# Narrow first FFN groups, one fp32 load, reordered loads, a DMA queue model and new durations in a statically scheduled attention + SwiGLU kernel

## The chip, the cores and the metric

One core of one Trainium2 chip. The metric is device time of one execution in microseconds (us); the median of several executions is quoted, and versions are compared by ratios of runs taken in the same rounds on the same chip. PE is TensorE, PEld its weight loads, DVE VectorE, ACT ScalarE, POOL GpSimd, SP SyncE.

## The reference, cut to what matters

```python
# q, k, v: [4, 8, 768, 64]; window 128, 4 sink keys; x: [3072, 512]
scores = q @ k.T / sqrt(64), kept where (key < 4) or (0 <= query - key < 128)
attn   = softmax(scores) @ v
x      = attn laid out as [tokens, heads * 64]
xn     = x / sqrt(mean(x * x) + 1e-6) * rms_g
out    = (silu(xn @ w_gate) * (xn @ w_val)) @ w_out      # 512 -> 1536 -> 512
```

The work is cut into 24 blocks of 128 tokens. Six groups of four blocks go through the FFN. For a block, attention needs its own q, k, v and those of its neighbour, and ends in `xr`, the normalized row block, which is transposed to `xnt` for the FFN.

## The kernel before: the parts concerned

The kernel does not issue instructions in the order in which it is written. It hands every piece of work to a `Plan` with a duration, what it needs and gives, and a priority. The plan plays the program through with these durations and so fixes each engine's order, once, when the program is built. On the chip every engine then works its list in order: when the first instruction of the list is not ready, the engine stands, whatever stands behind it.

```python
class Plan:
    def land(self, ring, at, work):              # when a DMA lands, as the plan believes
        others = max([v for r, v in self.rings.items() if r != ring], default=0)
        begin = max(at, self.rings.get(ring, 0))
        shared = min(work, max(0, others - begin))
        end = begin + work + shared
        ...
    def run(self):
        ...                                      # earliest start first, then priority
        free[e] = start + ns                     # ns: the duration given with the work
        if o["ring"] is not None:
            end = self.land(o["ring"], end, o["work"]) + 550
```

The loads and constants:

```python
    F32_LOADS = 2;  PE_MASKS = 2;  X_DMA_FROM = 8;  QK_DMA_FROM = 12
    GATE_LEAD = 3;  T_LEAD = 5;    GB_PRIO = -5
    # q0, q1 on SP, k0, k1 on ACT as fp32, cast by DVE; all others on GpSimd, cast by the DMA:
    for g in range(F32_LOADS): sw_block(g, "v")
    sw_w(0, 2); sw_block(2); sw_block(3)
    sw_w(2, 4); sw_w(4, 6); sw_w(6, 9); sw_w(9, 12)      # strips of w_gate and w_val
    sw_block(4); sw_wo(0, 6); sw_wo(6, 12)
    for g in range(5, NB): sw_block(g)
```

Some durations, and the FFN of a group (`ft` is one of twelve strips of 128 hidden columns; `ffn` needs `xnt` of every block in `cols`):

```python
    pe((240, 480, 590)[min(t, 2)], lambda: av(g, u), ...)       # ns
    dve(430, lambda: normal(g, u), ...)
    dve(1650, lambda: rms(g), ...)
    ...
    for G in range(NG):
        if G == 0:                                # one block at a time, four strips
            for tb in range(GB):
                for i in range(FTN // 4):
                    ffn(G, 3 * tb + i, range(4 * i, 4 * i + 4), slice(tb * P, (tb + 1) * P), ...)
        else:                                     # four blocks at once, one strip
            for ft in range(FTN):
                ffn(G, ft, (ft,), slice(0, GN), ...)
```

The softmax here doesn't subtract the row's maximum and nothing guards it: scores larger than these inputs give would overflow.

## Time and profile before

| | before |
|---|---|
| time, median of 4 runs | 257.19 us (256.48 to 257.77) |
| span of the profiled run (an execution of 257.9 us, 0.7 above the median) | 256.2 us |
| PE work, by columns at the spacing of the chain | 225.5 us |
| idle PE | 30.7 us |
| DVE, ACT, POOL busy | 183.6, 130.7, 93.1 us |

The table's PE work is not the busy time of the page: it is every listed matmul at the spacing that the chain shows (the prediction works it out). Its difference to the span is what a better order can win at most. The page's summary of the chain that ended last shows that a third of that chain is not PE. That third is no measure of idle PE (30.7 of 256.2 us): PE can have other work while the chain is on DVE.

```profile
PE 66%; DVE 21%; ACT 5%; issue 3%; DMA 2%; ACTq 0%; DVEq 0%
```

### The profile page before, as it was taken

To read this page: it belongs to the slowest core of one execution; us is meant where nothing else is said; L and a number is where in the kernel's file an instruction comes from. 1 tells how busy PE (TensorE), PEld (TensorE's weight loads), DVE (VectorE), ACT (ScalarE), POOL (GpSimd) and SP (SyncE) were. 2 spreads that over 40 slices of the span, in tenths; PEclk is the share of its full clock that TensorE was granted. 3 is DMA by queue.
4 is the path that set the end of the run, shared out by engine and by line. 5 is a ranking of instruction groups with operands and counts; after the bars stand their busy time and mean duration, and the time that the engine had idled before them with its cause. 6 is when DMAs were issued, how large, how long until landed. Compare 5 with 4: busy or idle time off the path is not lost.

```text
span 256.2 us, 5083 instructions
## 1 busy us (share of the span) xinstructions
PE 238.7 (93%) x1880; PEld 130.8 (51%) x1906; DVE 183.6 (72%) x481; ACT 130.7 (51%) x273; POOL 93.1 (36%) x128
## 2 busy tenths in 40 slices
PE   5788999989998999999989999999999989999994
PEld 1357997776544445344445444445455544444441
DVE  3577999599889998278997169998089984277600
ACT  2376463898835733446643455562564452333211
POOL 8984454989847464003303031013033310000000
PEclk9999999999999999999999999999999999999999
DMA  8999999999999999943303524301311112200012
GB/s 158 173 176 202 184 207 163 154 199 155 117 174 168 125 155 155 177 132 65 63 0 64 163 63 64 61 0 40 128 41 23 22 20 64 111 12 0 3 53 111
DMA packets 106970, 26.55 MB, mean 104 GB/s; under 512 B 97217, under 2 KB 103873, under 8 KB 106946
## 3 DMA queue, kind: packets, MB, share of 16 engines
q0 software_dynamic: 77568, 13.64, 71.6%
q1 hardware_dynamic: 27298, 12.07, 22.5%
q10 hardware_dynamic: 2080, 0.52, 1.1%
q8 instruction: 15, 0.25, 0.4%
q14 instruction: 9, 0.07, 0.1%
HBM read 28.31 MB, written 6.29 MB: 135 GB/s over the span
## 4 chain that ended last, share of the span: by engine, by line
PE 66%; DVE 21%; ACT 5%; issue 3%; DMA 2%; ACTq 0%; DVEq 0%
PE o L770 21%; PE g L737 19%; PE v L737 17%; DVE xr L547 4%; DVE p L750 3%; DVE r L543 3%; DVE hT L760 3%; DVE x L515 3%; ACT e L452 2%; PE s L439 2%; DMA stage<-in_k_dram 2%; PE av L503 2%; DVE e L469 2%; PE av L498 1%; ACT sq L523 1%
## 5 line engine op out<-in xcount | busy, mean ns | idle before, releaser
L737 PE MATMUL g<-xnt,wg 128*128 128x512 bf16 (+1 forms) x427 | 69.4, 307 | 3.7 <-DVE p L750 2.7
L737 PE MATMUL v<-xnt,wv 128*128 128x512 bf16 (+1 forms) x422 | 70.6, 306 | 0.6
L750 DVE SCALAR_TENSOR_TENSOR p<-th,g 128x512 bf16<-128x512 bf16 x72 | 48.0, 683 | 28.5 <-ACT th L744 28.5
L770 PE MATMUL o<-wo,hT 128*128 128x512 bf16 x278 | 65.6, 379 | 0.7 <-issue 0.3
L744 ACT ACTIVATE th<-g 128x512 bf16<-128x512 f32 x72 | 42.5, 599 | 34.2 <-PE g L737 31.9
L452 ACT ACTIVATE e<-s 128x512 bf16<-128x512 f32 (+1 forms) x100 | 47.2, 556 | 13.6 <-PE s L439 13.5
L737 PEld LDWEIGHTS <-wg 128*128 128x128 bf16 x432 | 33.9, 98 | 30.0 <-issue 4.8
L760 DVE TENSOR_TENSOR hT<-p,v 128x512 bf16<-128x512 bf16 x72 | 47.8, 682 | 1.9 <-PE v L737 1.3
L737 PEld LDWEIGHTS <-wv 128*128 128x128 bf16 x432 | 33.1, 98 | 24.0 <-issue 0.8
L474 POOL TENSOR_SCALAR_AFFINE_SELECT e<-e 128x512 bf16<-128x512 bf16 x20 | 12.6, 634 | 87.5 <-ACT e L452 60.5
L770 PEld LDWEIGHTS <-hT 128*128 128x128 bf16 x288 | 27.1, 98 | 30.9 <-issue 0.8
L523 ACT ACTIVATE sq<-x 128x512 bf16<-128x512 bf16 x24 | 15.1, 629 | 36.5 <-DVE x L515 36.4
L778 ACT ACTIVATE osb<-o 128x512 f32<-128x512 f32 x24 | 14.3, 606 | 26.0 <-PE o L770 26.0
L312 POOL DMA_DIRECT2D k<-in_k_dram x22 | 19.5, 889 | 11.9 <-DMA wo<-in_moe_w_out_dram 3.1
L316 POOL DMA_DIRECT2D v<-in_v_dram x24 | 21.4, 894 | 6.6 <-DMA q<-in_q_dram 3.8
L312 POOL DMA_DIRECT2D q<-in_q_dram x22 | 19.6, 891 | 7.4 <-DMA wo<-in_moe_w_out_dram 2.6
L515 DVE TENSOR_TENSOR x<-av,rden 128x256 bf16<-128x256 f32 x48 | 20.4, 425 | 1.7
L547 DVE SCALAR_TENSOR_TENSOR xr<-x,r,gb 128x512 bf16<-128x512 bf16 x24 | 18.4, 765 | 0.9
L503 PE MATMUL av<-v,e 128*128 128x65 bf16 x192 | 17.4, 197 | 1.1 <-DVE e L469 0.8
L503 PEld LDWEIGHTS <-e 128*128 128x128 bf16 x192 | 13.4, 101 | 4.7 <-DVE e L469 2.3
L498 PE MATMUL av<-v,e 128*128 128x65 bf16 x160 | 15.5, 195 | 0.0
L469 DVE TENSOR_TENSOR e<-e,masks 128x1024 bf16<-128x1024 bf16 (+1 forms) x24 | 14.9, 642 | 0.7 <-ACT e L452 0.6
(69 smaller groups left out, 181.3 us busy)
## 6 DMA issues: line engine op xcount, KB each, us to landing
out_dram<-osb SPq DMA_DIRECT2D x24, 256.0 KB, 2.0
v<-in_v_dram POOLq DMA_DIRECT2D x24, 128.0 KB, 9.1
q<-in_q_dram POOLq DMA_DIRECT2D x22, 128.0 KB, 9.8
k<-in_k_dram POOLq DMA_DIRECT2D x22, 128.0 KB, 9.0
wo<-in_moe_w_out_dram POOLq DMA_DIRECT2D x2, 768.0 KB, 15.3
wg<-in_moe_w_gate_dram POOLq DMA_DIRECT2D x3, 256.0 KB, 6.6
wv<-in_moe_w_val_dram POOLq DMA_DIRECT2D x3, 256.0 KB, 7.1
wg<-in_moe_w_gate_dram POOLq DMA_DIRECT2D x2, 384.0 KB, 11.1
```

The lines of the kernel that those rows point to most:

```text
L312: nc.gpsimd.dma_start(out=T[name, g], in_=block_of(src, g))
L316: nc.gpsimd.dma_start(out=V16[b][:, t, :, 0:D], in_=block_of(v, g))
L452: nc.scalar.activation(out=T["e", g, u][:, 2 * hi:2 * hi + 2, n0:n1, :].rearrange("p x n c -> p x (n c)"), in_=ps.rearrange("p (j c) -> p ...
L469: nc.vector.tensor_tensor(out=ev, in0=ev, in1=mv, op=ALU.mult)
L503: nc.tensor.matmul(out=dest, lhsT=T["e", g, u][:, x, 0, :], rhs=V16[b][:, t, h, :], start=(t == 0), stop=True, skip_group_check=True,)
L515: nc.vector.tensor_tensor(out=T["x16", g][:, 4 * u:4 * u + 4, :], in0=pvv[:, :, 0:D], in1=rden.unsqueeze(2).to_broadcast((P, 4, D)), op=AL ...
L547: nc.vector.scalar_tensor_tensor(out=T["xr", g], in0=T.pop(("x16", g)).rearrange("p h d -> p (h d)"), scalar=r[:, 3:4], in1=gb, op0=ALU.mu ...
L737: nc.tensor.matmul(out=ps[:, i * n:(i + 1) * n], lhsT=w_sb[:, kt, ft * P:(ft + 1) * P], rhs=T["xnt", G][:, kt, cols], start=(kt == 0), sto ...
L744: nc.scalar.activation(out=T["th", key], in_=BANK[("g", key)], func=ACT.Tanh, scale=0.5,)
L750: nc.vector.scalar_tensor_tensor(out=T["p1", key], in0=T.pop(("th", key)), scalar=1.0, in1=BANK.pop(("g", key)), op0=ALU.add, op1=ALU.mult,)
L760: nc.vector.tensor_tensor(out=T[hk][:, i:i + n, cols], in0=T.pop(("p1", key)).rearrange("p (n c) -> p n c", n=n), in1=BANK.pop(("v", key)) ...
L770: nc.tensor.matmul(out=BANK[("o", G, tb)], lhsT=T["h", G, ft // 4][:, ft % 4, tb * P:(tb + 1) * P], rhs=wo[:, ft, :], start=(ft == 0), sto ...
```

## The change: intent and diff

The intent: let the FFN of groups 1 and 2 start when two of their four blocks are ready; take fp32 casts off DVE; bring loads in the order of need; let the plan know that transposing DMAs queue behind the loads, and give it truer durations.

```diff
-    F32_LOADS = 2
-    PE_MASKS = 2
+    F32_LOADS = ("q0",)
+    LOADS = "k-0 v-0 qk-1 w-0-2 qkv-2 v-1 w-2-5 qkv-3 w-5-9 w-9-12 qkv-4 wo-0-6 qkv-5 wo-6-12 qkv-6 ..."
+    PE_MASKS = 3
-    X_DMA_FROM = 8
-    QK_DMA_FROM = 12
+    X_DMA_FROM = 10
+    QK_DMA_FROM = 10
-    GATE_LEAD = 3
-    T_LEAD = 5
+    GATE_LEAD = 2
+    T_LEAD = 3
-    GB_PRIO = -5
+    CHUNKS = (4,2,2)
+    GB_PRIO = -1200
     ...
     def land(self, ring, first, work):
+        r = self.rings
+        if ring == "POOL":                       # loads: behind each other and behind the fp32 load
+            r["POOL"] = max(first, r["POOL"], r["HW"]) + work
+            self.loads -= 1
+            return r["POOL"] + 520
+        ...
+        begin = max(first, r["TR"], r["POOL"])   # transposes and stores: behind the loads
     ...
-            dve(335, lambda: cast(n, g), ...)
+            act(640, lambda: cast(n, g, nc.scalar.copy), ...)
-            pe(270 * (n1 - n0) + 30, lambda: scores(g, *n), ...)
+            pe(220 * (n1 - n0), lambda: scores(g, *n), ...)
-            pe((240, 480, 590)[min(t, 2)], lambda: av(g, u), ...)
+            pe((130, 242, 354)[min(t, 2)], lambda: av(g, u), ...)
-            dve(430, lambda: normal(g, u), ...)
+            dve(548, lambda: normal(g, u), ...)
-        dve(1650, lambda: rms(g), ...)
+        dve(1745, lambda: rms(g), ...)
     ...
-        if G == 0: ...
-        else: ...
+        nc_ = CHUNKS[G] if G < len(CHUNKS) else 1
+        w, n = GN // nc_, 0
+        for c in range(nc_):
+            for ft in range(0, FTN, nc_):
+                ffn(G, n, range(ft, ft + nc_), slice(c * w, (c + 1) * w), p0 + 10 * n)
+                n += 1
```

Cut: bookkeeping of rings, durations of single loads, where the small GpSimd selects stand between the loads, and three added dependencies (the gb matmul waits for the first scores, a mask group for the transposes of its own q and k, the sink copy for the next block's scores). No run below takes the selects' places or these dependencies back.

More of the change, by code (lines that the diff above doesn't have):

```diff
@@ L27 @@
 class Plan:
+    LATE = 300
     HOP = {"PE": 40, "ACT": 35, "DVE": 35, "POOL": 90, "SP": 60}
@@ L36, in __init__ @@
     def __init__(self):
-        self.ops, self.given, self.rings, self.held = [], {}, {}, {}
+        self.ops, self.held = [], {}
+        self.rings = {"POOL": 0, "HW": 0, "TR": 0}
         self.banks = {i: 0 for i in range(8)}
@@ L45, in op, with land @@
         ))
-    def land(self, ring, at, work):
-        others = max([v for r, v in self.rings.items() if r != ring], default=0)
-        begin = max(at, self.rings.get(ring, 0))
-        shared = min(work, max(0, others - begin))
-        end = begin + work + shared
-        for r, v in self.rings.items():
-            if r != ring and v > begin:
-                self.rings[r] = v + shared
-        self.rings[ring] = end
-        return end
+    def land(self, ring, first, work):
+        r = self.rings
[3 more added lines that the diff above has]
+            return r["POOL"] + 520
+        if ring == "HW":
+            r["HW"] = max(first, r["HW"]) + work
+            return r["HW"] + 900
+        begin = max(first, r["TR"], r["POOL"])
+        if self.loads:
+            r["POOL"] = max(r["POOL"], first) + work
+            work *= 2
+        r["TR"] = begin + work
+        return r["TR"] + (350 if ring == "TR" else 650)
     def run(self):
-        free, given, users = dict(self.START), {}, {}
+        free, users = dict(self.START), {}
+        self.loads = sum(o["ring"] == "POOL" for o in self.ops)
         wait = {o["at"]: set(o["needs"]) for o in self.ops}
@@ L108, in run @@
             if o["ring"] is not None:
-                end = self.land(o["ring"], end, o["work"]) + 550
+                end = self.land(o["ring"], end, o["work"]) + self.LATE
             for s in o["drops"]:
@@ L158 @@
     inv_sqrt_d = 1.0 / math.sqrt(D)
-    F32_LOADS = 2
-    PE_MASKS = 2
+    F32_LOADS = ("q0",)
+    POOL_AT = (0,2,6)
+    DEPTH = 8
+    LOADS = "k-0 v-0 qk-1 w-0-2 qkv-2 v-1 w-2-5 qkv-3 w-5-9 w-9-12 qkv-4 wo-0-6 qkv-5 wo-6-12 qkv-6 qkv-7 qkv-8"
+    LOADS += "".join(f" qkv-{g}" for g in range(9, NB))
+    PE_MASKS = 3
     POOL_MASK_FROM = 12
-    X_DMA_FROM = 8
-    QK_DMA_FROM = 12
+    X_DMA_FROM = 10
+    QK_DMA_FROM = 10
     LD = 16
     GATE_FROM = 8
-    GATE_LEAD = 3
-    T_LEAD = 5
+    GATE_LEAD = 2
+    T_LEAD = 3
     SPLIT = (0,)
-    GB_PRIO = -5
+    CHUNKS = (4,2,2)
+    GB_PRIO = -1200
     const = ctx.enter_context(tc.tile_pool(name="const", bufs=1))
@@ L224, in sp @@
     def sp(ns, lat, fn, *args, **kw):
-        op({"SP": (ns, lat, fn)}, *args, ring="SP", **kw)
+        op({"SP": (ns, lat, fn)}, *args, **kw)
     dve(70, lambda: nc.vector.memset(ident, 0.0), gives=["id0"], prio=-99)
@@ L261, in spread_masks @@
         nc.vector.memset(masks[0:NS, 0, :, :], 1.0)
-    pool(270, make_ident, ["id0"], ["ident"], -90)
+    pool(270, make_ident, ["id0"], ["ident"], -89.2 + POOL_AT[0])
     for i in range(2):
         pool(270, lambda i=i: triangle(bias[:, i, :], NEG, i), ["bias0"],
-             [("bias", i)], -89.9 + i / 10)
+             [("bias", i)], -89.1 + POOL_AT[1] + i / 100)
         pool(330, lambda i=i: triangle(masks[:, 1, i, :], 0.0, i), ["masks0"],
-             [("masks1", i)], -81 + i / 10)
+             [("masks1", i)], -89.1 + POOL_AT[2] + i / 100)
     dve(220, cut_ident, ["ident"], ["idnos"], -50)
@@ L290, in make_headm @@
             )
-    pool(200, make_sel, ["sel0"], ["sel"], -80)
-    pool(180, lambda: make_headm(0), ["headm0"], ["headm1"], -79)
-    pool(180, lambda: make_headm(1), ["headm1"], ["headm"], -78)
+    pool(200, make_sel, ["sel0"], ["sel"], -89.1 + POOL_AT[2] + 1)
+    pool(180, lambda: make_headm(0), ["headm0"], ["headm1"], -89.1 + POOL_AT[2] + 2)
+    pool(180, lambda: make_headm(1), ["headm1"], ["headm"], -89.1 + POOL_AT[2] + 3)
     def block_of(src, g):
@@ L304, in load_f32, with cast @@
         eng.dma_start(out=T["st", name, g], in_=block_of(src, g))
-    def cast(name, g):
+    def cast(name, g, copy):
         T[name, g] = ld.tile([P, H, D], BF16, name=name)
-        nc.vector.tensor_copy(out=T[name, g], in_=T.pop(("st", name, g)))
+        copy(out=T[name, g], in_=T.pop(("st", name, g)))
     def load_bf16(name, src, g):
@@ L320 @@
     wo_src = moe_w_out.rearrange("(ft p) d -> p ft d", p=P)
-    sp(370, 1200, lambda: nc.sync.dma_start(
-        out=grow, in_=moe_rms_g.rearrange("(o d) -> o d", o=1)), (), ["grow"], -91, work=50)
-    for g in range(F32_LOADS):
-        sp(370, 1300, lambda g=g: load_f32("q", q, g, nc.sync), (), [("qst", g)], -90 + g,
-           work=900)
-        op({"ACT": (100, 1300, lambda g=g: load_f32("k", k, g, nc.scalar))}, (), [("kst", g)],
-           -90 + g, ring="ACT", work=900)
-        for n in "qk":
-            dve(335, lambda n=n, g=g: cast(n, g), [(n + "st", g)], [(n, g)], -9 + g)
+    for i, name in enumerate(F32_LOADS):
+        n, g = name[0], int(name[1:])
+        src, first, fn = q if n == "q" else k, i % 2 == 0, load_f32
+        if first:
+            op({"ACT": (450, 1000, lambda n=n, src=src, g=g: load_f32(n, src, g, nc.scalar))},
+               (), [(n + "st", g)], -90 + i, ring="HW", work=970)
+        else:
+            sp(400, 1000, lambda n=n, src=src, g=g: load_f32(n, src, g, nc.sync),
+               (), [(n + "st", g)], -90 + i, ring="HW", work=970)
+        act(640, lambda n=n, g=g: cast(n, g, nc.scalar.copy), [(n + "st", g), "table"],
+            [(n, g)], -99)
+    sp(400, 1000, lambda: nc.sync.dma_start(
+        out=grow, in_=moe_rms_g.rearrange("(o d) -> o d", o=1)), (), ["grow"], -89.5, ring="HW", work=50)
     act(1290, None, (), ["table"], -80)
@@ L336, in sw_load @@
         n = len(issue)
-        more = [("sw", n - 8)] if n >= 8 else []
-        op({"POOL": (ns, 1750, fn)}, list(needs) + more, list(gives) + [("sw", n)], -89 + n,
+        more = [("sw", n - DEPTH)] if n >= DEPTH else []
+        op({"POOL": (ns, 1720, fn)}, list(needs) + more, list(gives) + [("sw", n)], -89 + n,
            ring="POOL", work=work)
@@ L345, in sw_block @@
             if n == "v":
-                sw_load(lambda g=g: load_v(g), [("v", g)], 900)
+                sw_load(lambda g=g: load_v(g), [("v", g)], 910)
             else:
                 src = q if n == "q" else k
-                sw_load(lambda n=n, src=src, g=g: load_bf16(n, src, g), [(n, g)], 880,
+                sw_load(lambda n=n, src=src, g=g: load_bf16(n, src, g), [(n, g)], 860,
                         needs=[(n + "T", old)] if old >= 0 else [])
@@ L356, in sw_w @@
                 out=w_sb[:, :, cols], in_=src[:, :, cols]),
-                [(n, ft) for ft in range(f0, f1)], 650 * (f1 - f0), 740)
+                [(n, ft) for ft in range(f0, f1)], 663 * (f1 - f0), 740)
     def sw_wo(f0, f1):
@@ L361, in sw_wo @@
         sw_load(lambda: nc.gpsimd.dma_start(out=wo[:, rows, :], in_=wo_src[:, rows, :]),
-                [("wo", ft) for ft in range(f0, f1)], 650 * (f1 - f0), 810)
-    for g in range(F32_LOADS):
-        sw_block(g, "v")
-    sw_w(0, 2)
-    sw_block(2)
-    sw_block(3)
-    sw_w(2, 4)
-    sw_w(4, 6)
-    sw_w(6, 9)
-    sw_w(9, 12)
-    sw_block(4)
-    sw_wo(0, 6)
-    sw_wo(6, 12)
-    for g in range(5, NB):
-        sw_block(g)
+                [("wo", ft) for ft in range(f0, f1)], 663 * (f1 - f0), 810)
+    for what in LOADS.split():
+        n, *f = what.replace("-", " ").split()
+        if n == "w":
+            sw_w(int(f[0]), int(f[1]))
+        elif n == "wo":
+            sw_wo(int(f[0]), int(f[1]))
+        else:
+            sw_block(int(f[0]), n)
     def unit_gb():
@@ L385, in scale_gb @@
         nc.scalar.mul(gb, BANK.pop(("gb",)), C3)
-    pe(864, unit_gb, ["ones", "grow"], ["gbm"], GB_PRIO, takes=[("gb",)], mode=2)
+    pe(864, unit_gb, ["ones", "grow", ("s", 0, 0)], ["gbm"], GB_PRIO, takes=[("gb",)], mode=2)
     act(490, scale_gb, ["gbm", "table"], ["gb"], drops=[("gb",)])
@@ L646 @@
             else:
-                sp(1250, 1700, lambda n=n, g=g: dma_t(n, g),
-                   [(n, g)] + old + [("s", g - T_LEAD)], [(n + "T", g)], g, work=700)
+                sp(1290, 1200, lambda n=n, g=g: dma_t(n, g),
+                   [(n, g)] + old + [("s", g - T_LEAD)], [(n + "T", g)], g,
+                   ring="TR", work=1000)
         slots = [("s", g, u, hi) for u in range(2) for hi in range(2)]
@@ L653 @@
             pe(864, lambda g=g: mask_bias(g), [("bias", 0), ("bias", 1), "ident", "idnos"]
-               + ([("qp", g - 1)] if g else []), [("mb", g)], pa, takes=slots)
+               + ([("qp", g), ("kp", g)] if g else []), [("mb", g)], pa, takes=slots)
         for n0, n1 in parts:
@@ L658 @@
             last = (n0, n1) == parts[-1]
-            pe(270 * (n1 - n0) + 30, lambda g=g, n=(n0, n1): scores(g, *n), needs,
+            pe(220 * (n1 - n0), lambda g=g, n=(n0, n1): scores(g, *n), needs,
                [("s", g, n0)] + ([("s", g)] if last else []), pa + 1 + n0,
@@ L688 @@
             needs += [("av", g - 1, u)] if g else []
-            pe((240, 480, 590)[min(t, 2)], lambda g=g, u=u: av(g, u), needs, [("av", g, u)],
+            pe((130, 242, 354)[min(t, 2)], lambda g=g, u=u: av(g, u), needs, [("av", g, u)],
                pa + 5, takes=[("av", g, u)])
-            dve(430, lambda g=g, u=u: normal(g, u),
+            dve(548, lambda g=g, u=u: normal(g, u),
                 [("av", g, u)] + ([("xr", g - 3)] if g >= 3 else [])
@@ L696 @@
             early)
-        dve(1650, lambda g=g: rms(g),
+        dve(1745, lambda g=g: rms(g),
             [("ms", g), "gb"] + ([("xt", g - 3)] if g >= 3 else [])
@@ L709 @@
         else:
-            sp(1250, 1700, lambda g=g: dma_x(g), [("xr", g)] + old, [("xt", g)], g - 8, work=700)
+            sp(1290, 1200, lambda g=g: dma_x(g), [("xr", g)] + old, [("xt", g)], g - 8, ring="TR",
+               work=1000)
         if t == 0:
             dve(600, lambda b=b: sink_k(b),
-                [("kT", g)] + ([("ss", b - 2, i) for i in ((2, 4) if b - 2 < 2 else (2,))]
+                [("kT", g), ("s", g + 1)] + ([("ss", b - 2, i) for i in ((2, 4) if b - 2 < 2 else (2,))]
                                if b >= 2 else []), [("ksk", b)], 0.1 * g)
@@ L803 @@
         p0 = 1000.0 * G
-        if G == 0:
-            for tb in range(GB):
-                for i in range(FTN // 4):
-                    ffn(G, 3 * tb + i, range(4 * i, 4 * i + 4), slice(tb * P, (tb + 1) * P),
-                        p0 + 10 * (3 * tb + i))
-        else:
-            for ft in range(FTN):
-                ffn(G, ft, (ft,), slice(0, GN), p0 + 10 * ft)
+        nc_ = CHUNKS[G] if G < len(CHUNKS) else 1
[4 more added lines that the diff above has]
+                n += 1
         mine = [key for key in keys if key[0] == G]
@@ L815 @@
                 part = [("h", key) for key in mine if 4 * i <= key[1] < 4 * i + 4
-                        and (G or key[2] == tb * P)]
+                        and key[2] <= tb * P < key[2] + w]
                 pe(864, lambda G=G, tb=tb, i=i: project(G, tb, i),
@@ L825 @@
                 [("osb", G, tb)], drops=[("o", G, tb)])
-            sp(370, 1000, lambda G=G, tb=tb: store(G, tb), [("osb", G, tb)], [("st", G, tb)],
-               -100, work=700)
+            sp(400, 1000, lambda G=G, tb=tb: store(G, tb), [("osb", G, tb)], [("st", G, tb)],
+               -100, ring="ST", work=870)
     order = plan.run()
```

## The prediction

> **What bounds the kernel now.** I read the page first (engine shares, 40 slices), then the chain in order of time, the DMA view of the first 20 us, and engine sums in 16 us stretches.
>
> The page, engine shares and slices:
>
> ```profile
> PE 238.7 (93%) x1880; PEld 130.8 (51%) x1906; DVE 183.6 (72%) x481; ACT 130.7 (51%) x273; POOL 93.1 (36%) x128
> ...
> PE   5788999989998999999989999999999989999994
> ...
> DVE  3577999599889998278997169998089984277600
> ...
> DMA  8999999999999999943303524301311112200012
> ```
>
> PE looks full, but one 128x512 matmul is recorded as 379 ns while the chain spaces four of them at 0.86 us, so 0.215 us each. I therefore count PE work by columns: every matmul that the program lists, at the spacing the chain shows (0.215 us per 512 columns, 0.54 us for the eight score matmuls of a block, 0.03 us for a 65-column av). The sum is 225.5 us, 186 of it the three FFN products. The span is 256.2 us, so about 31 us are idle PE. To find where, I took each milestone's time from the trace and subtracted the PE work that stands ahead of it in program order: 13.5 us lost at the first g matmul (21.0 us minus 7.5), 15.0 when the third run of weight strips starts (30.5 minus 15.5), 15.5 at the first o (41.3), 19.3 at the first g of group 1 (71.0 minus 51.7), 21.7 at its first o (96.3), 22.8 and 24.0 at the same points of group 2, then only 2.9 more until the last matmul. The last 3.8 us are evacuation and store. So: **15 us at the start, 8.5 between 41 and 135 us, 3 later, 3.8 tail.** What fills the first two? The chain, cuts of it:
>
> ```profile
> 1.26 5.61 DMA stage<-in_k_dram
> ...
> 9.10 1.02 DVE q L308
> ...
> 11.90 1.82 PE s L421 x4
> ...
> 17.05 0.76 DVE xr L547
> ...
> 24.66 1.00 PE g L737 x16
> ...
> 53.02 0.75 DVE xr L547
> 55.10 0.76 DVE xr L547
> ...
> 69.27 0.75 DVE xr L547
> 70.02 0.61 DVE e L469
> 71.06 0.97 PE g L737 x4
> ```
>
> The reader is to see a serial beginning (fp32 q and k loads, casts, mask matmuls before av, normalization) and, from 45 to 71 us, DVE finishing xr of blocks 5 to 7, which the 512-column matmuls of group 1 wait for. The engine sums (columns PE, PEld, DVE, ACT, POOL) say DVE has no room then: 15.34 of 16 us, after 12.38 in the stretch before.
>
> ```profile
> 32.00:48.00 16.00, 15.79 (x223) 12.48 (x223) 12.38 (x29) 9.19 (x19) 9.66 (x12) 1.00 1.88 179
> 48.00:64.00 16.00, 14.97 (x223) 12.04 (x224) 15.34 (x46) 14.53 (x35) 14.63 (x17) 1.00 2.41 172
> ```
>
> The DMA view of 0 to 20 us:
>
> ```profile
> GB/s 0 0 0 17 134 274 287 267 218 217 219 217 212 170 155 156 175 198 187 193 201 185 156 154 156 154 156 154 154 156 153 161 191 197 193 200 197 193 199 196
> DMA packets 15089, 3.40 MB, mean 170 GB/s; under 512 B 12551, under 2 KB 15088, under 8 KB 15089
> ```
>
> Nothing moves before 1.5 us, then the DMA engines never rest: about 280 GB/s for fp32 blocks, 154 for cast blocks, 200 for weights.
>
> **What the Trainium skill says.** "Perfetto Trace Analysis", Identifying the Most-Contended Engine: matmul busy share is no measure of distance to the roofline, since matmuls are pipelined. Agrees: 379 ns recorded against 215 spaced. "TensorE: Matmul & The Clock Gate", Part 1: start to start is N/2.4 GHz + 2.5 ns warm (55.6 ns at 128 columns, 215.7 at 512), N/1.2 GHz cold. Agrees: sixteen 128-column matmuls in 0.89 us (56 ns), four 512-column ones in 0.86; the early mask group took 1.82 us, 455 ns each, so cold. That is why narrow chunks cost PE nothing. "DMA: Bandwidth & Descriptors", Issuing engines are not separate DMA queues: all issuers share the same 16 DMA engines. Agrees: busy tenths are 9 with one or three issuers. "Perfetto Trace Analysis", Optimization Strategy: where regimes change, interleaving them may help; that is what the chunks do.
>
> **The change part by part**, from the two programs' instruction order.
>
> *PE work.* Groups 1 and 2 get two chunks of 256 columns: 192 more matmuls and weight loads, same columns, 0 us by the spacing above. One more mask matmul group +0.86, two more x transposed on PE +0.43, blocks 10 and 11 of q and k no longer transposed there -0.86. Sum **+0.4 us**.
>
> *DVE and ACT.* The DVE casts of q0, k0, q1, k1 go (0.938, 0.564: 3.0 us), as do two masks of block 2 (0.686 each: 1.4); an fp32 copy of q0, an estimate of 0.6 us from the 0.59 us copies, goes to ACT. About 4 us of DVE work leave the first 25 us.
>
> *Head.* Before, first scores run at 10.7 us, and av of block 0 waits in program order behind mask group 1 until 13.5. After, q0 is the only fp32 load; at 280 GB/s its 0.26 MB are there near 3.7 us, and k0, second in line at 154 GB/s, near 5. Then q1 (issued about 3.7, landing at least 3.1 later as the fastest k load did), its transpose and copy, gb (2.07 us cold in the trace), the second half of the scores: av of block 0 near 9.8. The chain before needs 4.3 us from av to the transpose of xr, so x is ready near 14 instead of 17.9. But g and v need weight strips 0 to 4. Walking the queue with 0.94 us per fp32 block, 0.85 per cast block and 0.64 per weight strip of one matrix: before, 15.7 us of loads end with strips 2 and 3, at 17.6 from a start at 1.9, while 3.40 MB at 20 us put the same 3.15 MB at about 18.8; I add 1.2 us. After: q0 0.94, four blocks 3.4, four strips 2.56, four blocks 3.4, six strips 3.84: 14.1, so 17.2 for the last strip and 15.3 for its wg half. **First g near 16, not 21.** The gain then shrinks: the next strips (5 to 8) come behind block 3, at 22.3 and 24.9, and wg of strips 9 to 11 at 26.8. With 0.5 us to be seen, the third run of strips starts near 27.5 with 16.2 us of PE work ahead of it: 11.3 lost against 15.0. **Worth 3.5 us** (rounded down).
>
> *Chunks.* Group 1 starts on blocks 4 and 5. Adding DVE instructions in program order at their means, 61 us stand before xr of block 7 in the old program and 44 before xr of block 5 in the new one, while PE work ahead is alike (51.7 and 50.8). With that, DVE is ready by about 55 us (44, scaled by 0.91 for overlapping records as 183.6 union to 202 sum, plus some 14 idle), and PE would arrive at 51 + 12 = 63. So the 3.8 us lost there should fall to about 1.3: **worth 2.5**. From there through group 2's first o, 4.7 are lost; DVE work is only shifted earlier, so I give back a third: **1.5**. Later groups are unchunked and tail is same: 0.
>
> *Queue order, scheduler constants, DMA transposes from block 10 with shorter lead.* PE later lost only 2.9 us in 120, so I count 0.
>
> Sum: 3.5 + 2.5 + 1.5 - 0.4 = 7.1; 256.9 - 7.1 = **249.8 us**.
>
> **Rivals.** (1) *The weight stream takes the place of the fp32 loads*: three cast blocks cost 2.55 us where fp32 ones cost 2.8, so the same bytes gate group 0 and the start gains nothing but order. For it: DMA tenths of 9 until 109 us. Against: the old first g waited for xr, not for a landing. Then about 253. (2) *DVE stays the bound to 96 us*: chunks only move the wait from xr to hT, since DVE was at 15.2 of 16 again from 80 to 96. For it: p and hT need 1.2 us per 1.73 of PE, plus attention. Against: 4 us of DVE work gone and idle DVE before 48. Then about 252. (3) *All goes well*: block order and the truer queue model also close the later 2.9 us; then 246. (4) *Late transposes*: a lead of 3 blocks instead of 5 makes scores wait for landings, up to 9 us seen among them; 1 to 3 us back.
>
> **Range and chances.** Full effect 246, both rivals together about 255; 8 in 10 between 246 and 254. The 2% line is 251.8, two microseconds above my number, so faster 0.70, same 0.28, slower 0.02.
>
> **What would show it.** Right: first g near 16, 128-column g of strips 8 to 11 near 27.5, first 256-column g near 63 to 65, about 23 us idle PE in all, PE work 226. Wrong: first g waiting on weights beyond 19; DVE above 15 of 16 from 48 to 96 with g waiting on p; score matmuls waiting for transposed q or k after 80 us.

## The result, and the profile after

The changed kernel takes 250.26 us (249.8 to 250.32, 4 runs) against 257.19 us in the same rounds: ratio 0.9728, 95% interval 0.9699 to 0.9757. Ratios are the mean time of one kernel's fast runs over that of the other's fast runs of the same rounds, so not quite the ratio of the medians. The predicted time was 249.8 us, range 246 to 254. All four runs are fast ones at a granted clock of 0.997 or more.

The page of the changed kernel, in the order of the lines shown for before (shares, PE, DVE and DMA slices, chain):

```profile
PE 238.1 (96%) x2094; PEld 148.6 (60%) x2094; DVE 177.8 (72%) x470; ACT 133.2 (54%) x277; POOL 95.0 (38%) x129
...
PE   3998999999999999999999999999999999999993
...
DVE  2375879699899996599986089997279993377700
...
DMA  9999999999999999994122533212501102200022
...
PE 85%; DMA 8%; POOL 4%; issue 1%; ACT 0%; DVE 0%; POOLq 0%
```

DVE's share of the chain fell from 21% to nothing; its busy time fell by 5.8 us, but it is 72% of the span in both. PE's busy time is the same (238.7 and 238.1): busy time told nothing of the 7.7 us. The weight loads' busy time rose by 18 us for the 192 added ones, without any cost. The engine sums (PE, PEld, DVE, ACT, POOL, clock, DMA) of the stretches shown for before, and all waits of PE between 40 and 135 us:

```profile
32.00:48.00 16.00, 15.59 (x223) 12.20 (x221) 12.73 (x30) 11.04 (x23) 9.57 (x11) 1.00 1.86 181
48.00:64.00 16.00, 16.00 (x214) 12.02 (x213) 14.48 (x46) 13.88 (x32) 15.08 (x18) 1.00 2.38 166
```

The list of PE's waits for 40 to 135 us is empty. Where the idle time went, by the prediction's ledger (time of a milestone in the trace, minus the PE work ahead of it in program order, gives idle PE up to there):

| idle PE up to, us | before | after | saved in between |
|---|---|---|---|
| first g | 21.0 - 7.5 = 13.5 | 17.9 - 7.0 = 10.9 | 2.6 |
| third run of weight strips | 30.5 - 15.5 = 15.0 | 29.2 - 16.2 = 13.0 | -0.6 |
| first o of group 0 | 41.3 - 25.8 = 15.5 | 42.4 - 28.0 = 14.4 | -0.9 |
| first g of group 1 | 71.0 - 51.7 = 19.3 | 66.0 - 50.8 = 15.2 | 3.0 |
| first o of group 1 | 96.3 - 74.6 = 21.6 | 91.5 - 75.6 = 15.8 | 1.7 |
| first g of group 2 | 109.2 - 86.4 = 22.7 | 103.8 - 87.7 = 16.2 | 0.7 |
| first o of group 2 | 134.9 - 110.9 = 23.9 | 129.1 - 112.2 = 16.8 | 0.6 |
| last matmul | 252.4 - 225.5 = 26.9 | 244.6 - 225.9 = 18.7 | 1.1 |

(Each value is rounded by itself, so a difference can be 0.1 off, here and against the prediction's figures; the last column is taken from the rounded idle times.) The start gave little, 41 to 135 us gave 6.0, the rest 1.1. What changed at group 1 shows in the times of xr of blocks 6 and 7 and of the first g of group 1 (start, duration, engine, line, what), now:

```profile
63.10 0.75 DVE L560 SCALAR_TENSOR_TENSOR xr<-x,r,gb 128x512 bf16<-128x512 bf16 x1
65.99 1.91 PE L752 MATMUL g<-xnt,wg 128*128 128x256 bf16 x16
69.34 0.75 DVE L560 SCALAR_TENSOR_TENSOR xr<-x,r,gb 128x512 bf16<-128x512 bf16 x1
```

xr of block 7 is ready no earlier than before (70.1 us, 70.0 before), but the first g no longer waits for it: it starts at 66.0 us, not 71.0. The start's DMA view for 0 to 20 us explains part of how little the start gave:

```profile
GB/s 0 0 0 24 197 256 83 116 111 97 114 97 103 110 129 127 126 154 175 166 178 169 169 159 155 153 156 156 162 182 199 204 198 204 203 205 182 168 154 156
DMA packets 13252, 2.85 MB, mean 142 GB/s; under 512 B 11203, under 2 KB 13251, under 8 KB 13252
```

One column is 0.5 us. From 3.0 us on, when the single fp32 block is all but in (it lands at 3.6 us), the queue of cast loads moves 83 to 129 GB/s until 8.5 us, not 154; the kernel before moved 3.40 MB in these 20 us. The DMA busy tenths of the page read 9 all the while. The other part is the path of x of block 0, from its transpose to the first g:

```profile
16.59 0.39 PE L575 MATMUL x<-ident,xr 128*128 128x128 bf16 x4
17.01 0.42 DVE L581 COPY xnt<-x 128x512 bf16<-128x512 bf16 x1 [0.98 <-PE x L575]
17.86 1.06 PE L752 MATMUL g<-xnt,wg 128*128 128x128 bf16 x16
```

The copy to xnt ends at 17.43 us and the w_gate part that the first g needs lands at 17.62: both hold the first g, within 0.2 us of each other.

### The profile page after: what moved, and what is told of

It is laid out like the page before. It is cut to its first block, busy times and chain, and to the rows that moved or that the text cites. A ratio compares the mean times of both kernels' runs of the same rounds, so it can differ in the third digit from the quotient of the medians.

```text
span 248.5 us, 5479 instructions
## 1 busy us (share of the span) xinstructions
PE 238.1 (96%) x2094; PEld 148.6 (60%) x2094; DVE 177.8 (72%) x470; ACT 133.2 (54%) x277; POOL 95.0 (38%) x129
## 3 DMA queue, kind: packets, MB, share of 16 engines
q1 hardware_dynamic: 26306, 11.81, 22.7%
## 4 chain that ended last, share of the span: by engine, by line
PE 85%; DMA 8%; POOL 4%; issue 1%; ACT 0%; DVE 0%; POOLq 0%
PE o L785 25%; PE v L752 24%; PE g L752 23%; DMA k<-in_k_dram 5%; PE s L452 4%; DMA wv<-in_moe_w_val_dram 3%; PE av L516 2%; PE av L511 2%; PE av L501 1%; PE ss L618 1%; POOL v L331 1%; POOL k L327 1%; POOL q L327 1%; PE x L575 1%; PE k L412 1%
## 5 line engine op out<-in xcount | busy, mean ns | idle before, releaser
L752 PE MATMUL v<-xnt,wv 128*128 128x128 bf16 (+2 forms) x528 | 72.5, 282 | 0.3 <-DMA wv<-in_moe_w_val_dram 0.3
L752 PE MATMUL g<-xnt,wg 128*128 128x128 bf16 (+2 forms) x528 | 70.3, 282 | 0.1
L752 PEld LDWEIGHTS <-wg 128*128 128x128 bf16 x528 | 43.1, 98 | 19.5 <-issue 1.6
L465 ACT ACTIVATE e<-s 128x512 bf16<-128x512 f32 (+1 forms) x100 | 48.4, 551 | 10.2 <-PE s L452 10.1
L752 PEld LDWEIGHTS <-wv 128*128 128x128 bf16 x528 | 42.4, 98 | 18.2 <-issue 1.1
L785 PEld LDWEIGHTS <-hT 128*128 128x128 bf16 x288 | 26.9, 98 | 30.0 <-issue 0.8
L487 POOL TENSOR_SCALAR_AFFINE_SELECT e<-e 128x512 bf16<-128x512 bf16 x20 | 13.8, 697 | 80.9 <-ACT e L465 54.6
L793 ACT ACTIVATE osb<-o 128x512 f32<-128x512 f32 x24 | 14.5, 603 | 26.1 <-PE o L785 25.9
L327 POOL DMA_DIRECT2D q<-in_q_dram x23 | 20.6, 895 | 11.6 <-DMA wo<-in_moe_w_out_dram 3.2
L327 POOL DMA_DIRECT2D k<-in_k_dram x24 | 21.4, 892 | 8.7 <-DMA v<-in_v_dram 3.0
L536 ACT ACTIVATE sq<-x 128x512 bf16<-128x512 bf16 x24 | 15.2, 632 | 16.7 <-DVE x L528 16.4
L452 PE MATMUL s<-qkT 64*128 64x256 bf16 (+1 forms) x200 | 14.4, 266 | 0.8 <-DVE qkT L419 0.5
L511 PE MATMUL av<-v,e 128*128 128x65 bf16 x160 | 14.8, 193 | 0.0
L527 DVE RECIPROCAL rden<-av 128x4 f32<-128x4 f32 x48 | 8.4, 176 | 8.1 <-PE av L516 8.0
```

The costliest lines, as they stand in the source:

```text
L327: nc.gpsimd.dma_start(out=T[name, g], in_=block_of(src, g))
L452: nc.tensor.matmul(out=BANK[slot][:, j * 256 + n0 * P:j * 256 + n1 * P], lhsT=qkT[pr, 1, hp, t * P:(t + 1) * P], rhs=qkT[pr, 0, hp, (t + n ...
L465: nc.scalar.activation(out=T["e", g, u][:, 2 * hi:2 * hi + 2, n0:n1, :].rearrange("p x n c -> p x (n c)"), in_=ps.rearrange("p (j c) -> p ...
L511: nc.tensor.matmul(out=dest, lhsT=T["e", g - 1, u][:, x, 1, :], rhs=V16[b][:, t - 1, h, :], start=(t == 1), stop=False, skip_group_check=True,
L752: nc.tensor.matmul(out=ps[:, i * n:(i + 1) * n], lhsT=w_sb[:, kt, ft * P:(ft + 1) * P], rhs=T["xnt", G][:, kt, cols], start=(kt == 0), sto ...
L785: nc.tensor.matmul(out=BANK[("o", G, tb)], lhsT=T["h", G, ft // 4][:, ft % 4, tb * P:(tb + 1) * P], rhs=wo[:, ft, :], start=(ft == 0), sto ...
```

## The experiments

Twelve kernels were run, each correct and each timed against the kernel before on its chip. A word on what such a run can say: every edit makes the plan lay out all engines anew. Taking a part out shows what the rest is worth without it, not what the part is worth by itself, and the values do not add up. The runs are from several sessions on different chips; the kernel before took 257.19 us beside the changed kernel and 256.85, 256.57 and 256.52 beside the others, so a difference of two medians of the table can be 0.7 us off. The ratios are not touched by this.

| kernel | time, us | ratio to before (95%) |
|---|---|---|
| changed | 250.26 | 0.9728 (0.9699 to 0.9757) |
| changed, no chunks | 257.7 | 1.0021 (1.0006 to 1.0036) |
| before, only chunks | 255.96 | 0.9962 (0.9941 to 0.9982) |
| changed, old loads | 250.6 | 0.9744 (0.9714 to 0.9775) |
| changed, old queue model | 255.13 | 0.9925 (0.9897 to 0.9952) |
| changed, six old constants | 252.67 | 0.9842 (0.9822 to 0.9862) |
| changed, old queue model, q and k by DMA from block 12, lead 5 | 252.02 | 0.9817 (0.9794 to 0.9840) |
| changed, old durations | 257.5 | 1.0030 (1.0014 to 1.0047) |
| changed, chunks in group 1 alone | 259.7 | 1.0113 (1.0090 to 1.0136) |
| before, only durations | 259.47 | 1.0121 (1.0082 to 1.0160) |
| before, chunks and durations | 256.26 | 0.9993 (0.9976 to 1.0010) |
| changed, k0 as fp32 too | 249.64 | 0.9705 (0.9679 to 0.9731) |
| changed, four fp32 blocks | 250.38 | 0.9752 (0.9728 to 0.9776) |

The theory at the outset was the prediction's: chunks about 4 us, head about 3.5, queue model and constants nothing. Its rivals were that chunks help only together with other parts, and that the plan's knowledge is the gain.

### No chunks

```diff
-    CHUNKS = (4,2,2)
+    CHUNKS = (4,)
```

> The changed kernel with groups 1 and 2 in one piece of four blocks again, all else as changed. Theory (chunks bring what was saved between the first o of group 0 and the first o of group 2, where idle PE time grew by 8.4 us before and by 2.4 after): the time goes back by 4 to 6 us, to 254 to 256 us, and the idle PE time before the first g of group 1 is again above 18 us. Rival (less DVE work, new load order and scheduler did it): it stays below 252 us and the first g of group 1 still has about 15 us of idle PE before it.

Measured 257.7 us: all of the gain is gone. The timeline of this kernel shows the wait that the theory named, on the transpose of x and the first g of group 1 (start, duration, engine, line, what; in brackets the idle time and what ended it):

```profile
70.00 0.61 PE L575 MATMUL x<-ident,xr 128*128 128x128 bf16 x4 [1.36 <-DVE xr L560]
71.28 1.01 PE L752 MATMUL g<-xnt,wg 128*128 128x512 bf16 x2 [0.67 <-ACT xnt L581]
```

Idle PE before the first g of group 1 is 19.6 us, as in the kernel before (19.3), though loads, durations and DVE work are those of the changed kernel. The rival falls for this stretch: without chunks the other parts save nothing here. The size was above the theory's (4 to 6 us), because 2.8 more are lost up to the first o of group 1.

### Only chunks

```diff
-        if G == 0: ...
-        else: ...
+        # the chunk loops of the changed kernel, CHUNKS = (4,2,2)
```

> The kernel before with the chunks of two blocks in groups 1 and 2 and nothing else. Theory (chunks are most of the gain): 251 to 253 us. Rival (chunks help only when the blocks come earlier and DVE has been relieved): 255 us or more.

Measured 255.96 us, 0.4% faster than before. The theory that chunks are most of the gain by themselves falls, and the rival's number holds. The first g of group 1 comes at 68.0 us with 50.3 us of work ahead: 17.7 idle, of which 3.9 arose after the first o of group 0, as many as before (3.8). xr of block 5, all that the chunk needs, was done at 54.2 us: the plan had placed the g later than it had to. This run also shows how much one profile's start is worth: every instruction up to there is the same as in the kernel before, and still 13.3 us were idle at the third strip run instead of 15.0. The changed kernel has such repeats too: without chunks, and with chunks in group 1 alone, every engine's list is the same up to the first g of group 1, and 13.5 and 14.8 us are idle at the third strip run, where the changed kernel has 13.0 (first g at 18.3 and 19.7 us, not 17.9). So the 2.0 us that the changed kernel seemed to save there is hardly more than the difference between two executions of one list.

### Old loads

```diff
-    F32_LOADS = ("q0",)
-    LOADS = "k-0 v-0 qk-1 w-0-2 qkv-2 v-1 w-2-5 qkv-3 w-5-9 w-9-12 qkv-4 wo-0-6 qkv-5 wo-6-12 ..."
+    F32_LOADS = ("k0", "q0", "k1", "q1")
+    LOADS = "v-0 v-1 w-0-2 qkv-2 qkv-3 w-2-4 w-4-6 w-6-9 w-9-12 qkv-4 wo-0-6 wo-6-12 qkv-5 ..."
```

> The changed kernel with the loads of before: q0, k0, q1, k1 as fp32 on two hardware queues, the others in the old order; the fp32 casts stay on ACT. The prediction valued the head at 3.5 us, which would give 253.8. The trace of the changed kernel shows 2.0 us less idle PE at the third run of weight strips and only 1.1 at the first o, so the theory now is 250.5 to 252 us: the new order pays about 1 us. If the fp32 loads were the better choice and only the order paid, it is below 250.

Measured 250.6 us; its interval and that of the changed kernel overlap for most of their width. The new loads are worth 0.3 us by the medians, which these runs cannot tell from nothing. First g comes at 20.3 us instead of 17.9, but 1.4 us more PE work stands ahead of it, and at the first o of group 0 it has less idle PE (13.6) than the changed kernel (14.4).

### Old queue model

```diff
-    LATE = 300
+    LATE = 550
-    def land(self, ring, first, work): # new
+    def land(self, ring, at, work):    # old
```

> The changed kernel with the old model of the DMA queues in the scheduler (landing times only; engine durations and all constants stay as changed). Theory: the model places few instructions differently, 250 to 251.5 us. Rival (the truer model is what removed idle time in the later groups, 1.1 us, and part of the middle): 252 to 254 us.

Measured 255.13 us: the rival wins, by more than it claimed. Up to the first g of group 1 nothing differs (15.5 idle), then 6.1 us are lost before the first o. The chain of this kernel names the cause (start, duration, what):

```profile
64.60 9.41 DMA qkT<-q
74.02 0.14 issue
74.15 0.90 PE ss L611 x4
75.06 0.42 PE x L568 x4
75.48 2.90 PE g L745 x16
```

A transposing DMA of q was issued at 64.6 us while the cast loads still filled the queues, and took 9.4 us to land. Run without a chip, the plan of this kernel.py gives the time that it believed in: 4.9 us from issue to landing, where the plan of the changed kernel has 11.0. So it put the sink scores (ss), which read that q, early in PE's list, at 67.9 us of its own time instead of 74.3, and PE stood until 74.15. The wait list of PE for 60 to 80 us has this one entry (total, times, longest):

```profile
PE ss L611 <- DMA qkT<-q: 3.5, 1, 3.5
```

The next g matmuls were slower, 2.90 us for sixteen of 256 columns where 1.75 is usual; the mean granted clock from 72 to 80 us was 0.79, with 0.58 and 0.57 in the two stretches from 74 to 78. In the changed kernel transposes take as long, issued between 60 and 80 us and, for comparison, between 112 and 130, when the loads are done (landing, min/median/max):

```profile
DMA to landing us min/median/max: 7.7/8.5/9.6
DMA to landing us min/median/max: 2.4/2.5/4.2
```

but there the plan expects it, and PE does other work meanwhile. The new model is not exact either: for the first six of them it expects 9.2 to 13.8 us.

### Old queue model with transposes out of its way

```diff
 (on top of the old queue model)
-    QK_DMA_FROM = 10
+    QK_DMA_FROM = 12
-    T_LEAD = 3
+    T_LEAD = 5
```

> The old queue model again, but q and k by DMA transpose only from block 12 and with a lead of 5 blocks, as before. In the run with the old model alone PE stood 3.5 us (5.5 with the weight load ahead of it) for a transposed q that took 9.4 us to land, between the first g and the first o of group 1. Theory (that wait is nearly all the new model is worth): the wait is gone and the time is 250.5 to 252 us. Rival (the model matters throughout): 253.5 us or more.

Measured 252.02 us, the theory's upper edge. The wait is gone, 15.4 us idle at the first g of group 1 and 16.1 at the first o. So 3.1 of the 4.9 us that the old model cost came from the blocks whose transposes it misjudged; of the 1.8 left, 0.9 is PE work (226.8 against 225.9) for the blocks transposed there. By the ratios, which leave out the difference between chips, the steps are 5.1 us for the old model and 2.3 for what is left.

### Six old constants

```diff
-    PE_MASKS = 3;  X_DMA_FROM = 10;  QK_DMA_FROM = 10;  GATE_LEAD = 2;  T_LEAD = 3;  GB_PRIO = -1200
+    PE_MASKS = 2;  X_DMA_FROM = 8;   QK_DMA_FROM = 12;  GATE_LEAD = 3;  T_LEAD = 5;  GB_PRIO = -5
```

> The changed kernel with six small constants as before: two mask groups on PE, x by DMA transpose from block 8, q and k by DMA transpose from block 12, lead of 5 blocks, gate lead 3, gb early. Chunks, loads, queue model and durations as changed. Theory (chunks plus the queue model carry the gain, the constants little): 250.5 to 252.5 us. Rival (relieving DVE of the masks and of copies is what chunks need): 253 us or more, with the loss before the first g of group 1.

Measured 252.67 us, just above what the theory allowed and below the rival: the constants are worth 2.4 us by the medians. By the ratios it is 2.9 us, which would be 253.1 beside the changed kernel, the rival's lower edge; so neither is settled. The loss is not in one place: 1.2 us more idle than the changed kernel at the first o of group 0, 1.8 at the first g of group 1, 2.3 at the first o of group 2, 2.7 at the end. Which of the six does it was not tried.

### Old durations

```diff
-            pe(220 * (n1 - n0), ... scores)
+            pe(270 * (n1 - n0) + 30, ... scores)
-            pe((130, 242, 354)[min(t, 2)], ... av)
+            pe((240, 480, 590)[min(t, 2)], ... av)
-            dve(548, ... normal)
+            dve(430, ... normal)
-        dve(1745, ... rms)
+        dve(1650, ... rms)
```

> The changed kernel whose scheduler has the old durations of score, av, normalization and rms work; these set the order only. Theory: order of a few instructions, 250 to 251.5 us. Rival (with av counted at about twice its duration the plan puts the chunks too late, as in the run with chunks alone): 253 us or more, with idle PE above 17 us before the first g of group 1.

Measured 257.5 us: the rival wins, and four durations that no instruction carries decide over 7.2 us. 1.5 us more are idle at the first o of group 0 than in the changed kernel, 3.2 us are lost between the first o of group 0 and the first g of group 1 (0.8 in the changed kernel), 4.1 from there to the first o of group 2 (1.6), 3.4 after (1.9). The trace of the kernel before already says which numbers are right. Its chain, for one normalization (four steps) and one rms chain:

```profile
49.83 0.10 DVE rden L514
49.95 0.42 DVE x L515
50.38 0.10 DVE rden L514
...
52.02 0.07 DVE m L530
...
53.02 0.75 DVE xr L547
53.77 0.34 DVE qkT L406
```

From one rden to the next are 0.55 us where the old plan has 0.43; from m to the end of xr 1.75 where it has 1.65. An av half block with sinks is one piece of 0.11 and eight of 0.03, 0.35 us, where the old plan has 0.59. The old plan took PE's attention for slower and DVE's for faster than they are. That it therefore put work that depends on DVE too early among PE's is an explanation that fits and is not shown: PE's waits in this trace are many and short (the longest after the first mask matmuls is 0.9 us), and none of the four was tried alone.

### Chunks in group 1 alone

```diff
-    CHUNKS = (4,2,2)
+    CHUNKS = (4,2)
```

> The changed kernel with chunks in group 1 alone; group 2 in one piece. Theory (the wait that chunks remove is that of the first g of group 1 for xr of block 7): 250 to 251.5 us. Rival (both groups share it): 252.5 to 254 us, with 2 us more idle PE between the first o of group 1 and the first o of group 2.

Measured 259.7 us, the slowest of the edits of the changed kernel, and above the rival's range. Up to the first o of group 1 all is well (17.0 idle); 6.5 us go before the first g of group 2. PE's waits from 100 to 115 us:

```profile
PE g L752 <- DMA xnt<-xr: 4.0, 1, 4.0
PE av L516 <- DVE e L482: 1.7, 2, 1.3
```

In this kernel x of blocks 10 and 11 is transposed by DMA, and a group in one piece waits for the last of them: xr of block 11 was done at 103.5 us, its transpose issued at 103.7 and landed at 111.3, and g started at 111.5. In the changed kernel the first chunk reads blocks 8 and 9, which PE transposes. So, for 4.0 of these 6.5 us, the chunk of group 2 hides a DMA wait, not the DVE wait that the prediction had in mind.

### Only durations

```diff
 (kernel before)
-    old four durations
+    new four durations
```

> The kernel before with the four corrected durations in its scheduler (score, av, normalization, rms) and nothing else. Taking them out of the changed kernel cost 7.2 us. Theory (durations and chunks pay only together: without chunks group 1 still waits for xr of block 7): 254.5 to 257 us. Rival (the durations are the gain by themselves): 250 to 252 us.

Measured 259.47 us, 1.2% slower than before. With truer durations the plan still made PE's list such that it met a transpose of x whose input was late (wait list of PE):

```profile
PE x L562 <- DVE xr L547: 6.1, 3, 4.4
```

24.5 us are idle before the first g of group 1 (19.3 before). The profiled execution took 261.87 us, the other three 259.22 to 259.61, so some of this belongs to that execution alone. The rival falls, and the theory's range was too kind: truer durations without chunks do harm.

### Chunks and durations

```diff
 (kernel before)
+    chunk loops, CHUNKS = (4,2,2), and the new four durations
```

> The kernel before with chunks and corrected durations, but with its loads, its queue model, its masks and its leads. Theory (these two parts together are the core of the gain): 251 to 253 us, and not more than 16.5 us of idle PE before the first g of group 1. Rival (queue model and constants are needed as well): 254.5 us or more.

Measured 256.26 us, the same as before within 0.3%. My second theory, that these two are the core, falls too; the rival wins. 18.5 us idle before the first g of group 1, and PE still stood 3.2 us for xr in three places.

### More fp32 blocks

```diff
-    F32_LOADS = ("q0",)
-    LOADS = "k-0 v-0 qk-1 w-0-2 ..."
+    F32_LOADS = ("q0", "k0")                  # second run: ("q0", "k0", "q1", "k1")
+    LOADS = "v-0 qk-1 w-0-2 ..."              # second run: "v-0 w-0-2 ..."
```

> The changed kernel with k0 as fp32 too, on the second hardware queue, so that the software queue starts with v0. In the changed kernel the software queue's first loads moved only about 110 GB/s from 3 to 9 us, one block per 0.9 us of GpSimd issue time and the selects between, where the kernel before moved over 200. Theory (the start is bound by issue on GpSimd): q1, k1 and the weight strips land 0.8 to 1 us earlier, first g 0.5 to 1 us earlier, 249.3 to 250 us. Rival (two fp32 loads share the engines and delay the first scores): 250.3 us or more.

> The changed kernel with q0, k0, q1 and k1 as fp32 on the two hardware queues, cast on ACT, the rest in the new order. Theory (start bound by issue on GpSimd): weight strips 0 to 4 land about 2 us earlier and first g comes before 17.5 us, 248.8 to 249.8 us. Rival (four fp32 blocks share the DMA engines, q0 and k0 land later and ACT casts delay the first exponentials): 250.3 to 251.5 us.

Two blocks: 249.64 us, the lowest median of all, but its interval overlaps that of the changed kernel, so a gain is not shown. One of its five runs (253.0) was 1.8% above its fastest and its profile fell in the slow state, so that trace is not read here. Four blocks: 250.38 us, no gain. The fast trace of the four-block run shows the faster loads that the theory forecast: 3.41 MB moved in the first 20 us instead of 2.85, and the w_gate and w_val parts that the first g and v need landed at 16.4 and 18.4 us instead of 17.6 and 19.6. But q0 landed at 4.4 us instead of 3.6, the first g came at 18.1 us (17.9), and at the first o of group 0 the idle time is the same, 14.2 against 14.4. The first g did not wait for these weights: the copy of x of block 0 to xnt ended at 17.8 us, 1.5 us after they had landed. So in this order the path of x holds the first g, and faster loads alone do not move it.

## Why the prediction was right or wrong, point by point

**The bound: right.** Idle PE was the thing to win. The ledger's total came out as told, about 23 us of idle PE (22.6) with 226 us of PE work (225.9), and the narrow chunks cost PE nothing: eight 256-column matmuls take 0.87 us and four of 512, as many columns, 0.86.

**Head, "Worth 3.5 us": wrong in size.** The ledger has 1.1 at the first o of group 0, no more than repeats of the same instructions differ by, and undoing the loads costs 0.3 us, not distinguishable from zero. Two steps failed. One is the walk of the queue at 0.85 us per cast block from 1.9 us on: until 8.5 us only 83 to 129 GB/s moved, and the wg half told for 15.3 us landed at 17.6. The other is the path of x of block 0, told for 14 us: av came at 10.9 instead of 9.8, the transpose of xr stood behind the third mask group in PE's list until 16.6, and xnt was ready at 17.4. (The 3.1 us to landing that the prediction took for the fastest k load is that of a transposing DMA; the fastest k load from GpSimd took 6.7. q1 then took 3.9.) First g was told for 16 and came at 17.9 us, third strips for 27.5 and came at 29.2. The rival "the same bytes gate group 0 and the start gains nothing but order" describes the outcome better, though bytes were only one of the two gates. That GpSimd's issue is what holds the early rate fits the run with four fp32 blocks; it was not isolated, as the share of small packets changes too.

**Chunks, 2.5 + 1.5 us: mechanism right, size too small, and not by themselves.** Between the first o of group 0 and the first g of group 1 idle time grows by 0.8 instead of 3.8 us (1.3 was told); up to group 2's first o by 1.6 instead of 4.6 (two thirds of 4.7 was told, 3.1). So 6.0 us where 4.0 were told. The first g of group 1, told for 63 to 65 us, came at 66.0. Without chunks the wait for xr of block 7 is back, and 7.4 us with it. Rival (2), DVE stays the bound to 96 us, did not come true: DVE was busy 14.5 to 14.6 of 16 us in each stretch from 48 to 96 us, and PE's list of waits is empty there. (Its 1.2 us for p and hT is the plan's figure; the trace has 0.68 us for each.) For group 2 the wait that chunks remove is another one than I had named, the DMA transposes of x.

**"Queue order, scheduler constants, DMA transposes ...: I count 0": wrong.** This is the failed step with the largest terms. Taken out of the changed kernel one at a time, the queue model costs 4.9 us, the four durations 7.2, the six constants 2.4; the loads near 0. I did not even list the durations. The rival "late transposes" was the right wait, up to 9.4 us to land, but the changed plan knew of it and the old one did not. I had valued what the parts do to the engines' work. The queue model and the durations do nothing there; their worth lies in what PE meets next in its list.

**The later groups: 0 told, 1.1 found.** The sum was right (249.8 told, 250.26 measured) because a head too large by more than 2 us stood against a middle and an end too small by 3.1. That is luck in the sizes, not in the bound.

**What stays open.** Single parts give 0.4% (chunks), -1.2% (durations), 0.1% (both), so the gain belongs to the combination, but I have not shown which smallest set has it. Much of each removal's cost may be that the remaining constants were chosen for the whole; the runs do not separate a part's own worth from a layout that no longer fits. The plans, run without a chip, narrow it: for the end of the last matmul the plan of the changed kernel says 242.4 us (244.6 in the trace), without chunks 248.6 (252.1), with chunks in group 1 alone 251.0 (254.2), but with the old queue model 242.1 (250.2) and for chunks and durations in the kernel before 243.1 (251.1). So most of what chunks are worth the plan itself foresees, while in the last two the plan looks as good as the whole change and the chip does not follow it; in the last, 4 of the 8 us between plan and trace are there at the first g (17.3 against 21.3).

## What to carry to other kernels

When engines work fixed lists in order, count the work ahead of each milestone and subtract it from the milestone's time: the ledger shows which stretch has time to win, while busy time of PE was the same to 0.6 us in two kernels 7.7 us apart. Before scheduling by durations, compare each one with the trace: a wrong one costs no instruction and can still cost 3%. Correcting some and leaving others is no sure gain, though: the four durations alone made the kernel before 1.2% slower. So compare the plan's own times with the trace, milestone by milestone, too. And test combinations, since here no part nor pair tried in the kernel before gave more than 0.4%, and the whole gave 2.7%.

## What the Trainium skill lacked or had wrong

- "TensorE: Matmul & The Clock Gate", Back-to-back issue gap, gives about 81 ns at 128 columns and 131 ns at 512 for a stream of weight loads and matmuls. Here, in such a stream, sixteen of 128 columns take 0.89 us (56 ns) and four of 512 take 0.86 us (215 ns). Part 1 of the same page, which calls for 55.6 and 215.7, holds.
- "DMA: Bandwidth & Descriptors", SWDGE vs HWDGE vs iDMA, says that an engine goes round-robin between its queues. It has no figure for a transposing DMA issued while the software queue is full: 7.7 to 9.6 us to landing for one 128x512 block of q or k, against 2.4 to 4.2 after the loads.
- The same page, Bandwidth, has no row for cast loads in pieces of 64 elements (128 bytes as the trace counts them): steady 154 GB/s (of bf16 written), 83 to 129 in the first microseconds when the queue is just being filled. DMA busy share is 9 tenths of the page's slices in both.
- No page has a figure for how much the loads and casts at the start of one and the same instruction list differ between executions: 1.7 and 1.8 us of idle PE at 30 us, with casts of q0 on DVE of 0.41 and 0.86 us in two executions of one list (of q1 0.83 and 1.01).
